# GpSimd takes over part of the weight conversion and of the float16 halves from ScalarE, and the first 680 pieces of the order are written anew

## The chip, the core and the metric

The kernel runs on one core of a Trainium2 chip. The metric is the device time in microseconds, the median of several runs. Five engines work side by side, each through a queue of its own that it empties in order: TensorE (PE, matmuls), VectorE (DVE), ScalarE (ACT), GpSimd (POOL) and SyncE (SP, which here only issues transfers). [...]

## The reference

Eight batches of an attention with 32 memory slots give x (4608 x 512, from q, k, v and phi), and two products with the gate h - tanh(h) between them follow:

```python
a = softmax(phi over the 576 positions)
k_m, v_m = a^T k, a^T v                     # 32 slots for each of 8 heads
x = softmax(q k_m^T / 8) v_m                # per head, then heads side by side
h = x @ w_in                                # 4608 x 512 @ 512 x 2048
out = (h - tanh(h)) @ w_out                 # @ 2048 x 512
```

w_in and w_out come as float64; all else is float32.

## The kernel before

The 4608 tokens are 18 units u of 256, and the 2048 hidden columns are 4 blocks fb of 512. For each batch b the product v_m w_in is formed first (steps `P`), so that one step `H u.fb` multiplies attention weights by it and gives h, and `M u.fb` adds one block of the second product. Every float32 operand of these products is split into two float16 halves, "high" and "low" (the rest), and three products of halves stand for one of floats. The halves of the weights are made once, at the start, from 32 raw blocks of 128 x 512 float64 values (i0 to i15 of w_in, o0 to o15 of w_out), taken in 16 pairs p.

All work stands in one order written out by hand as the string `ORDER`: about 1,700 pieces, read from left to right. A piece is a letter code with numbers, and a piece that is named several times goes on at each naming to its next part. The order of the pieces is the order of every engine's queue, and SP's too. The codes that matter here:

- `i3:pp5`, `o1:gg`: load a raw block, or a pair of blocks, into the buffer of that tag. `FX b` loads phi by rows (L151), `KA b` and `KB b` load k and v, `Q b.t` loads q. Blocks with the tag gg share a ring of three buffers.
- `T p`: converts a pair to float32. Its first part reads the top 16 bits of each value and writes them into the tile top (L453, ScalarE). Its second part joins them with shifted low words (L457, VectorE). Its third part writes the high half (L470, ScalarE).
- The low half of a pair: `Lv p` on VectorE (L481); `L p` scales on ScalarE (L493) and subtracts on GpSimd (L495); `Lp p` on TensorE (L487, L488) with a copy on ScalarE (L490).
- `X b`, `YX b`, `XT b`, `XU b`: maximum of phi (VectorE, L226), exponentials (ScalarE, L231), transposes on TensorE (L240, L251), each with a copy on ScalarE (L243, and L255 for the tail). `V b.r` pools k and v with them (TensorE, L267, L275). `N`, `U`, `S`, `AM`, `AE`, `AD`, `AT`, `AS` follow up to the halves of the attention weights. `AMv`, `ADv`, `ASv` are the same with VectorE in GpSimd's place.
- After `H`: the square (ScalarE, L633), `a` or `ap` (VectorE L646, ScalarE L648, VectorE L650), `g` the high half of the gate (ScalarE, L670), and `c` (GpSimd, L676) or `cv` (VectorE, L676) its low half.
- `Z0.0`: two matmuls whose result nobody reads (L862).

PSUM tiles of the steps rotate over two slots h0, h1 and a third tile pa; a piece that ends in x swaps the two kinds. The tile top has one buffer, under the tag us.

Of the kernel before, what the change touches and what calls it, by code (L numbers as in the profile page):

```python
# [81 lines left out]
H2.0x AT1.1 PL1.1 g0.1 FX2 Q2.1 OP1 ASv1.1 H2.0 T4 OP1 a2.0 X2 ASv1.1 c0.1 L5 FA2 i12:kv2 o11:gg i14:kv3 M0.1 H2.1 T12 OP0 H2.1 XP2 M0.1 a2.1 H3.0 H3.1x  # L82
Y2 CWv1 o14:kv3 o12:kv2 Q2.0 FA3 a2.0 a2.0 a2.1 OP0 T4 g2.0 c2.0 a2.1 YE2 T12 g2.1 W0 T12 M2.0 H3.0 c2.1 H3.1 T13 M2.0 M2.1 a3.0 a3.1 Lv12 Lv4
T13 V2.0 V2.1 P0.2x P1.2x a3.0 a3.1 OP2 T6 P0.2 a3.0 T6 N2 a3.1 PL0.2 g3.0 T13 W2 Lv13 M2.1 T7 H1.2x H0.2 g3.1 P1.2 T6 OP2 T7 c3.1 H1.2
H0.2 T7 c3.0 PL1.2 a1.2 a0.2 Lv7 Lv6 M3.0 U2x M3.0 M3.1 P0.3 T15 M3.1 a0.2 UV2 OP3 T15 BS0 a0.2 P0.3 g0.2 a1.2 PL0.3 a1.2 H1.3 H0.3x T14 g1.2
OP3 H1.3 U2 T15 M0.2 c0.2 M0.2 T14 ap1.3 cv1.2 ap1.3 H0.3 ap1.3 a0.3 UV2 S2.1x S2.0x P1.3 H2.2 S2.1 g1.3 T14 L14 P1.3 a0.3 L15 H2.2 S2.0 AM2.0 PL1.3
a0.3 M1.2 H2.3x H3.2 M1.2 c1.3 AM2.0 P2.0 L14 L15 M1.3 P2.1 M1.3 ap2.2 AE2.0 ap2.2 g0.3 H2.3 ap2.2 AMv2.1 AD2.0 a2.3 c0.3 AD2.0 BF0 H3.2 a2.3 P2.0 BH0 g2.2
BL0 a2.3 PL2.0 AMv2.1 AT2.0 ap3.2 cv2.2 R1 FQ3 P2.1 O1 O1 AE2.1 ap3.2 ap3.2 PL2.1 BS1 BF1 AS2.0 AS2.0 M0.3 M0.3 H4.0 H4.0 ap4.0 R0 P2.2 H3.3 g2.3 c2.3
O0 O0 BH1 BL1 AD2.1 AD2.1 ap4.0 ap4.0 M2.2 R2 X3 g3.2 c3.2 P2.2 PL2.2 H3.3 H4.1 H4.1 ap3.3 ap3.3 g4.0 ap4.1 ap4.1 KR3.0 XP3 Y3 f4.0 s4.0 M2.2 QT3.0
ap3.3 g3.3 s4.0 YE3 cv4.0 M2.3 M2.3 H4.2 O2 O2 c3.3 ap4.1 AT2.1 R3 H4.2 BS2 P2.3 AS2.1 P2.3 g4.1 AS2.1 V3.0x PL2.3 ap4.2 ap4.2 BF2 BH2 M3.2 f4.1 ap4.2  # L90
f4.2 M3.2 H4.3x s4.1 KR3.1 s4.1 BL2 V3.1 N3 k4:q XX M3.3 M3.3 H4.3 ap4.3 ap4.3 g4.2 U3x U3 UV3 M4.0 M4.0 cv4.1 UV3 S3.0x ap4.3 O3 O3 P3.0 M4.0
M4.0 S3.0 AMv3.0 P3.0 M4.1 H5.0 BS3 AMv3.0 AE3.0 f4.3 k0:e g4.3 cv4.3 M4.1 M4.1 M4.1 PL3.0 c4.2 s4.2 s4.2 P3.1 H5.0 a5.0 a5.0 M4.2 sv4.3 H5.1 CW4 BF3 a5.0
BH3 BL3 H5.1 g5.0 k2:q c5.0 M4.2 M4.2 f5.0 QT3.1 M4.2 H5.2 s5.0 sv4.3 M4.3 P3.1 a5.1 ADv3.0 a5.1 M4.3 M4.3 PL3.1 S3.1 ADv3.0 s5.0 a5.1 AT3.0 M4.3 H5.2 S3.1
E4 g5.1 a5.2 a5.2 E4 CW2 f5.1 E4 E4 sv5.1 P3.2 M4.3 H5.3 H5.3 FQ4 M5.0 FA4 M5.0 a5.2 cv5.1 E4 E4 AS3.0 a5.3 sv5.1 M5.0 M5.0 CW0 AS3.0 H6.0
M5.1 M5.1 M5.1 M5.1 f5.2 a5.3 g5.2 KR4.0 cv5.2 s5.2 s5.2 a5.3 H6.0 a6.0 f5.3 a6.0 a6.0 P3.2 H6.1 s5.3 H6.1 f6.0 M5.2 M5.2 M5.2 M5.2 P3.3 g5.3 c5.3 s5.3
M5.3 ap6.1 ap6.1 PL3.2 H6.2 ap6.1 g6.1 P3.3 AM3.1 AM3.1 c6.1 AE3.1 X4 XP4 g6.0 M5.3 c6.0 s6.0 PL3.3 f6.1 H6.2 a6.2 KR4.1 M5.3 Ev5 Ev5 M5.3 s6.0 Ev5 Ev5
Ev5 a6.2 ADv3.1 ADv3.1 YM4 M5.3 s6.1 Ev5 a6.2 YM4 YE4 H6.3 H6.3 s6.1 QT4.0 AT3.1 ap6.3 ap6.3 M6.0 M6.0 AS3.1 AS3.1 g6.2 k3:e f6.2 M6.0 sv6.2 V4.0 M6.1 M6.1
ap6.3 g6.3 f6.3 M6.0 M6.1 M6.1 sv6.3 sv6.2 H7.0 H7.0 a7.0 c6.2 V4.1 N4 W3 a7.0 sv6.3 M6.2 SI0 H7.1 a7.0 f7.0 H7.1 a7.1 U4 UV4 FQ5 UV4 M6.2 QT4.1
M6.2 a7.1 M6.2 U4 H7.2 H7.2 SSv0 NI0 a7.1 f7.1 a7.2 c6.3 M6.3 NI0 g7.0 a7.2 a7.2 s7.0 S4.0 c7.0 S4.0 AMv4.0 M6.3 M6.3 E6 s7.0 g7.2 c7.2 H7.3 H7.3
E6 a7.3 M6.3 E6 s7.1 E6 E6 W4 g7.1 M6.3 E6 s7.1 P4.0 P4.0 S4.1x S4.1 AMv4.1 a7.3 X5 CW3 AMv4.0 AE4.0 a7.3 g7.3 M7.0 M7.0 M7.0 M7.0 H8.0 H8.0  # L100
f7.2 c7.1 M7.1 M7.1 M7.1 M7.1 s7.2 f7.3 PL4.0 ap8.0 ap8.0 AMv4.1 AD4.0 ap8.0 XP5 s7.2 k5:e sv7.3 CW5 cv7.3 M7.2 KR5.0 AD4.0 f8.0 g8.0 M7.2 M7.2 M7.2 sv7.3 AE4.1
ADv4.1 s8.0 s8.0 c8.0 AT4.0 H8.1 YM5 ADv4.1 H8.1 P4.1 P4.1 M7.3 M7.3 a8.1 a8.1 a8.1 H8.2 AS4.0 PL4.1 M7.3 Ev7 H8.2 a8.2 FA5 QT5.0 YM5 a8.2 YE5 f8.1 M7.3
Ev7 P4.2 P4.2 g8.1 M7.3 AS4.0 c8.1 s8.1 s8.1 Ev7 Ev7 a8.2 g8.2 Ev7 H8.3 M8.0 Ev7 M8.0 c8.2 M8.0 V5.0 M8.1 AT4.1 AS4.1 KR5.1 PL4.2 H9.0 H8.3 a8.3 a8.3
a8.3 H9.0 f8.2 a9.0 a9.0 s8.2 s8.2 M8.1 M8.1 V5.1 f8.3 P4.3x P4.3 N5 s8.3 k6:e M8.0 M8.1 g8.3 H9.1x H9.1 a9.0 PL4.3 U5x s8.3 UV5 ap9.1 f9.0 M8.2 M8.2
UV5 ap9.1 ap9.1 c8.3 f9.1 M8.2 M8.2 M8.3 g9.0 c9.0 M8.3 SI1 k7:q SS1 U5 S5.0 g9.1 M8.3 sv9.0 k8:e E8 E8 H9.2 E8 E8 S5.0 M8.3 M8.3 AS4.1 H9.2
H9.3x sv9.0 CW6 ap9.2 ap9.2 ap9.2 QT5.1 c9.1 M9.0 M9.0 M9.0 E8 E8 s9.1 s9.1 AM5.0 H9.3 a9.3 AM5.0 f9.2 a9.3 FQ6 a9.3 NI1x NI1 AE5.0 AD5.0 AD5.0 H10.0x H10.0
M9.1 M9.1 a10.0 s9.2 P5.0 f9.3 S5.1x a10.0 g9.2 P5.0 c9.2 a10.0 M9.0 M9.1 H10.1 s9.2 CW8 M9.1 M9.2 g9.3 c9.3 S5.1 AMv5.1 AMv5.1 AE5.1 M9.2 M9.2 M9.2 AT5.0 AS5.0
X6 XP6 s9.3 H10.1 s9.3 M9.3 PL5.0 ap10.1 H10.2 AS5.0 ADv5.1 ap10.1 ap10.1 g10.1 f10.1 g10.0 YM6 f10.0 H10.2 a10.2 FA6 P5.1 P5.1 c10.0 CW7 YM6 PL5.1 M9.3 a10.2 a10.2
QT6.0 M9.3 M9.3 M9.3 s10.0 E9 E9 s10.1 H10.3x KR6.0 H10.3 H11.0 cv10.1 a10.3 E9 E9 E9 E9 a10.3 a10.3 YE6 P5.2 P5.2 s10.0 M10.0 M10.0 M10.0 KR6.1 V6.0 H11.0
# [1035 lines left out]
```

## Time and profile before

| | us |
|---|---|
| median of 3 runs | 633.12 |
| lowest and highest run | 632.84, 633.73 |
| the profiled execution, its own time | 633.45 |
| span in its profile, first to last instruction | 631.7 |

The span is 1.75 us shorter than the time of its own execution, and that execution is 0.33 us above the median. Every time of a row counts from the start of the span. In the notation `out<-in xcount` a number in square brackets is the time that the engine stood idle before the first instruction of the row, with what ended it.

### The profile page before, as it was taken

To read this page: it belongs to the slowest core of one execution; us is meant where nothing else is said; L and a number is where in the kernel's file an instruction comes from. 1 tells how busy PE (TensorE), PEld (TensorE's weight loads), DVE (VectorE), ACT (ScalarE), POOL (GpSimd) and SP (SyncE) were. 2 spreads that over 40 slices of the span, in tenths; PEclk is the share of its full clock that TensorE was granted. 3 is DMA by queue.
4 is the path that set the end of the run, shared out by engine and by line. 5 is a ranking of instruction groups with operands and counts; after the bars stand their busy time and mean duration, and the time that the engine had idled before them with its cause. 6 is when DMAs were issued, how large, how long until landed. Compare 5 with 4: busy or idle time off the path is not lost.

```text
span 631.7 us, 16308 instructions
## 1 busy us (share of the span) xinstructions
PE 618.8 (98%) x6924; PEld 487.2 (77%) x6924; DVE 546.1 (86%) x714; ACT 447.0 (71%) x623; POOL 344.1 (54%) x309
## 2 busy tenths in 40 slices
...
GB/s 341 400 371 357 152 204 146 164 40 68 189 141 166 39 95 60 67 147 128 100 117 91 140 41 156 102 90 173 38 46 168 123 102 79 56 147 34 167 101 39
DMA packets 25872, 85.02 MB, mean 135 GB/s; under 512 B 2752, under 2 KB 2752, under 8 KB 25024
## 3 DMA queue, kind: packets, MB, share of 16 engines
...
## 4 chain that ended last, share of the span: by engine, by line
PE 83%; DVE 9%; DMA 5%; ACT 1%; issue 1%; SPq 0%; POOL 0%; DVEq 0%; ACTq 0%; POOLq 0%
PE h L626 26%; PE x L773 22%; PE o L773 16%; PE o L754 7%; PE o1h L754 3%; PE pp L579 3%; DMA q<-in_qt_dram 2%; PE pkv L267 2%; DMA raw<-in_w_in_dram 1%; PE psc L319 1%; DMA raw<-in_w_out_dram 1%; DVE h L646 1%; DVE h L650 1%; DVE bw L713 1%; DVE bw L706 1%
## 5 line engine op out<-in xcount | busy, mean ns | idle before, releaser
L626 PEld LDWEIGHTS <-ph 128*128 128x128 f16 x2304 | 178.1, 98 | 20.2 <-issue 4.4
L676 POOL TENSOR_TENSOR g<-h,g 128x512 f16<-128x512 f32 x112 | 123.7, 1128 | 109.1 <-ACT g L670 109.1
L697 POOL TENSOR_TENSOR f<-s,f 128x512 f16<-128x512 f32 x86 | 107.9, 1276 | 84.5 <-ACT f L693 74.1
L773 PEld LDWEIGHTS <-f 128*128 128x128 f16 x1344 | 129.2, 98 | 20.2 <-issue 5.2
L626 PE MATMUL h<-ah,ph 128*128 128x256 f16 (+3 forms) x1536 | 138.7, 246 | 0.6 <-DVE h L646 0.6
L773 PE MATMUL x<-bt,f 128*128 128x256 f16 x1008 | 128.3, 273 | 0.0
L648 ACT ACTIVATE u<-u,beta 128x1024 f32<-128x1024 f32 x72 | 82.3, 1145 | 44.5 <-DVE h L646 44.3
L646 DVE SCALAR_TENSOR_TENSOR h<-h,u 128x1024 f32<-128x1024 f32 x72 | 87.8, 1222 | 26.6 <-ACT u L633 22.6
L633 ACT ACTIVATE u<-h 128x1024 f32<-128x1024 f32 x72 | 73.1, 1019 | 51.2 <-PE h L626 32.6
L773 PEld LDWEIGHTS <-g 128*128 128x128 f16 x1008 | 97.9, 98 | 14.7 <-issue 3.5
L650 DVE SCALAR_TENSOR_TENSOR h<-u,h 128x1024 f32<-128x1024 f32 x72 | 94.0, 1307 | 15.9 <-ACT u L648 15.7
L670 ACT ACTIVATE g<-h 128x512 f16<-128x512 f32 (+2 forms) x128 | 68.1, 579 | 14.7 <-DVE h L650 8.5
L626 PE MATMUL h<-al,ph 128*128 128x256 f16 (+3 forms) x768 | 75.1, 246 | 0.5 <-DVE al L570 0.5
L754 PEld LDWEIGHTS <-g 128*128 128x128 f16 x384 | 36.9, 98 | 43.7 <-issue 2.5
L693 ACT ACTIVATE f<-s 128x1024 f16<-128x1024 f32 x56 | 58.6, 1048 | 11.1 <-DVE s L686 7.0
L754 PE MATMUL o<-wout_hi,g 128*128 128x512 f16 x192 | 59.1, 379 | 0.0
L684 DVE TENSOR_TENSOR s<-h 128x512 f32<-128x512 f32 x56 | 45.7, 816 | 1.6
L773 PE MATMUL o<-wout_hi,f 128*128 128x256 f16 x224 | 45.9, 273 | 0.0
L773 PE MATMUL x<-wout_hi,g 128*128 128x256 f16 x224 | 45.8, 273 | 0.0
L773 PE MATMUL o<-wout_hi,g 128*128 128x256 f16 x224 | 45.8, 273 | 0.0
L773 PE MATMUL o<-bt,g 128*128 128x256 f16 x336 | 45.3, 273 | 0.0
L592 ACT ACTIVATE ph<-pp 128x1024 f16<-128x1024 f32 x32 | 32.5, 1015 | 12.8 <-PE pp L579 11.8
...
## 6 DMA issues: line engine op xcount, KB each, us to landing
...
raws<-in_w_in_dram SPq DMA_DIRECT2D x6, 1023.5 KB, 10.3
...
```

Of the source, the lines that this page charges most:

```text
L626: nc.tensor.matmul(hp[:, k, tu : tu + w], st[b]["p"][fb][i][:, g, cs], st[b][ax][:, g, ta : ta + w], start=(n == 0 and k % 2 == 0 and m == ...
L633: nc.scalar.activation(uu, hp, AF.Square, scale=1.0 / (S_A * S_P))
L646: nc.vector.scalar_tensor_tensor(t, hp, C2 * S_G / (S_A * S_P), uu, op0=ALU.mult, op1=ALU.mult)
L648: nc.scalar.activation(uu, uu, AF.Square, bias=c["beta"])
L650: nc.vector.scalar_tensor_tensor(h3, uu, CC, t, op0=ALU.add, op1=ALU.mult)
L670: nc.scalar.activation(hi, x, AF.Copy)
L676: eng.tensor_tensor(lo[:, ks], x[:, ks], hi[:, ks], op=ALU.subtract)
L684: nc.vector.tensor_tensor(s[:, 0:2], pair, a_block(h3, 0, 0).unsqueeze(1).to_broadcast((P, 2, 2, P)), op=ALU.add)
L693: nc.scalar.activation(f[:, 0], s, AF.Copy)
L697: eng.tensor_tensor(f[:, 1, ks], s[:, ks], f[:, 0, ks], op=ALU.subtract)
L754: nc.tensor.matmul(o, gx[:, k, P * tt : P * tt + P], wx[:, 4 * fb + k, :], start=(first and k == 0 and wx is wout_hi and gx is gh), stop=( ...
L773: nc.tensor.matmul(dst, a(na, kk), b(nb, kk), start=(new and kk == 0 and na == 0 and nb == 0), stop=(end and kk == 1 and na == 1))
```

## The change

Three things change.

- The first part of nine `T` (pairs 1, 2, 3, 7, 8, 9, 12, 14, 15) becomes a copy on GpSimd (`Tg`). The high half is cut off from `T` and becomes a piece of its own, `J` on ScalarE (12 pairs) or `Jg` on GpSimd (pairs 2, 6, 8, 13). Eight `g` (0.1, 0.3, 1.0, 1.3, 2.0, 2.1, 3.0, 3.1) become `gq`, copies on GpSimd. The tile top gets a second buffer under the tag bw, for pairs 2, 3, 8 and 10.
- The first 490 words of the order are replaced by 484 others; the 1,206 words from `N3 k4:q XX` on stay. Apart from the above, in the new words `L` remains for pairs 11 and 12 alone (before: 2, 5, 10, 11, 14, 15), `Lv` has eleven pairs (before seven), `cv` takes the place of `c` for 0.3, 3.0 and 3.1, some `AM`, `AD` and `AS` change between VectorE and GpSimd, four `a` become `ap` and two `ap` become `a`, and there are 15 `Z0.0` (before 28).
- The loads are issued in another order. Ahead of `Q0.0` stand the same loads as before.

```diff
-TOP = ("us",)
+TOP = ("us", "bw")
+TOP_B = (2, 3, 8, 10)
 
 ORDER = """
-i1:gg FX0 i0:gg Z0.0 T0 X0 i6:kv3 i2:gg i3:pp5 T0 i4:kv2 Z0.0 Z0.0 Z0.0 Z0.0 Z0.0 Z0.0 Z0.0 KA0 KB0 o2:gg Z0.0 YX0 T3 T0 o3:gg Z0.0 Z0.0 Z0.0 Z0.0 XT0 Z0.0
-Z0.0 T3 XU0 XT0 T1 T3 T1 Z0.0 Lp0 T2 XU0 T1 Lp3 Z0.0 Z0.0 Z0.0 V0.0 T2 Lv1 Z0.0 Z0.0 V0.1 Lp0 T2 L2 Lp3 T9 L2 N0 T9
-Q0.0 Q0.1 Z0.0 U0 Z0.0 UV0 U0 UV0 Z0.0 S0.0 T9 P0.0x S0.1 S0.0 AM0.0 AM0.0 P0.1 S0.1 AMv0.1 P0.0 P0.1 AE0.0 AMv0.1 AE0.1 AD0.0 AD0.0 AD0.1 AD0.1 AT0.0 PLp0.0
-PLp0.1 Z0.0 AT0.1 PLp0.1 Z0.0 Lp9x Z0.0 o6:gg o4:gg o5:pp2 i10:kv3 KB1 o7:gg PLp0.0 T10 ASv0.0 FX1 Lp9 ASv0.1 T10 ASv0.0 H0.0 ASv0.1 T10 T11 T11 H1.0x o10:pp5 o0:pp2 o1:gg
-L10 H0.0 KA1 i8:kv2 Q1.0 Q1.1 o8:gg KA2 o9:pp4 k1:q H1.0 KB2 H1.1 X1 YX1 L10 XT1 H0.1 T8 XU1 Z0.0 a0.0 a1.0 T8 a0.0 XT1 T8 XU1 V1.0 a0.0
-Lv8 V1.1 a1.0 g0.0 a1.0 M0.0 cv0.0 H1.1 ap1.1 N1 U1 M0.0 H0.1 g1.0 ap1.1 T11 UV1 U1 S1.0 ap1.1 UV1 a0.1 L11 S1.0 S1.1x T5 g1.1 a0.1 c1.0 L11
-S1.1 P1.1x P1.0 M1.0 AMv1.0 T5 T5 AM1.1 AMv1.0 P1.0 AE1.0 T4 L5 AM1.1 c1.1 PL1.0 AD1.0 AD1.0 AE1.1 AD1.1 AT1.0 W1 P1.1 ASv1.0 a0.1 ASv1.0 AD1.1 M1.0 M1.1 M1.1
...
+i1:gg i3:pp5 FX0 i0:gg i6:kv3 i4:kv2 i2:gg T0 KB0 KA0 o2:gg o3:gg Tg3 T0 X0 Tg3 Q0.0 J0 YX0 Tg2 J3 Tg1 Tg2 Q0.1 Lp0x Z0.0 Z0.0 Z0.0 Z0.0 XT0
+XU0x Z0.0 Z0.0 Lp3 Z0.0 Jg2 Tg1 Tg9 XT0 XU0 J1 Lp0 Lp3 Lv2 Lv2 Lv1 Lv1 Z0.0 Z0.0 V0.0 V0.1 N0 Z0.0 U0x Z0.0 UV0 U0 Z0.0 S0.0x Tg9
+UV0 S0.0 AM0.0 AM0.0 P0.0x S0.1x S0.1 AM0.1 P0.1x AM0.1 P0.0 J9 AE0.0 P0.1 AE0.1 AD0.0 AD0.0 AD0.1 AD0.1 AT0.0 AT0.1 o5:pp2 o4:gg o7:gg KA1 o6:gg Q1.1 Lp9x PLp0.1 PLp0.0
+Z0.0 Z0.0 T10 Lp9 ASv0.0 T10 ASv0.0 PLp0.0 H0.0x FX1 PLp0.1 ASv0.1 ASv0.1 J10 o1:gg T11 o0:pp2 Tg8 H0.0 H1.0 H1.1 Lv10 Lv10 T11 H1.0 o9:pp4 Q1.0 KB1 X1 a0.0
+a1.0 YX1 Tg8 i8:kv2 o10:pp5 i10:kv3 KB2 o11:gg FQ3 XT1 Jg8 H0.1 XU1 a0.0 XT1 a0.0 a1.0 XU1 Z0.0 V1.0 g0.0 H1.1 J11 V1.1 Lv8 Lv8 a1.0 M0.0 cv0.0 ap1.1
...
-    def to_f32(p, ts):
+    def to_f32(p, ts, pool):
 
         r = [raws.pop(2 * p + i) for i in range(2)]
         if "top" not in c:
             c["top"] = [big.tile([P, 2, 512], U32, tag=TOP[i], name=f"top{i}", bufs=1) for i in range(len(TOP))]
             for x in c["top"]:
                 nc.gpsimd.memset(x, 0)
-        top = c["top"][0]
-        c["top"].append(c["top"].pop(0))
+        top = c["top"][p in TOP_B]
         if len(r[0].shape) == 3:
             parts = [(r[0], top, ts)]
         else:
...
         dims = {2: ("p (f w) -> p f w",), 3: ("p i (f w) -> p i f w",)}
         for x, g, t in parts:
             e = dims[len(x.shape)][0]
-            nc.scalar.activation(g.bitcast(F16).rearrange(e, w=2)[..., 1], x.bitcast(BF16).rearrange(e, w=4)[..., 2], AF.Copy)
+            half, bits = g.bitcast(F16).rearrange(e, w=2)[..., 1], x.bitcast(BF16).rearrange(e, w=4)[..., 2]
+            if pool:
+                nc.gpsimd.tensor_copy(half, bits)
+            else:
+                nc.scalar.activation(half, bits, AF.Copy)
         yield
         for x, g, t in parts:
             e = dims[len(x.shape)][0]
...
 
     tfs, his = {}, {}
 
-    def conv(p):
+    def conv(p, pool=False):
 
         ts = big.tile([P, 2, 512], U32, tag="ss", name=f"wt{p}")
-        yield from to_f32(p, ts)
-        yield
+        yield from to_f32(p, ts, pool)
         tfs[p] = ts.bitcast(F32)
+
+    def high(p, pool=False):
         his[p] = half_of(p, win_hi, wout_hi)
-        nc.scalar.activation(his[p], tfs[p], AF.Copy, scale=S_W)
+        if pool:
+            nc.gpsimd.tensor_scalar(his[p], tfs[p], S_W, None, op0=ALU.mult)
+        else:
+            nc.scalar.activation(his[p], tfs[p], AF.Copy, scale=S_W)
 
     def half_of(p, win, wout):
         f, o = 2 * p % 4, 2 * p - 16
...
         return half_of(p, win_lo, wout_lo)
 
     def low(p):
+        yield
         nc.vector.scalar_tensor_tensor(low_of(p), tfs[p], S_W, his[p], op0=ALU.mult, op1=ALU.subtract)
 
     def low_pe(p):
...
             (a_block(h3, 1, 0), [a_block(gg[:, n], 1, 0) for n in range(2)]),
         )
 
-    def a_high(u, fb):
+    def a_high(u, fb, pool=False):
         gs[u, fb] = big.tile([P, 2, 4, UT], F16, tag="gg", name=f"g{u}{fb}", bufs=3)
         for x, (hi, _) in a_parts(u, fb):
-            nc.scalar.activation(hi, x, AF.Copy)
+            if pool:
+                nc.gpsimd.tensor_copy(hi, x)
+            else:
+                nc.scalar.activation(hi, x, AF.Copy)
 
     def a_low(u, fb, eng):
         for x, (hi, lo) in a_parts(u, fb):
...
         "AD": lambda b, t: att.soft_div(b, st[b], t), "ADv": lambda b, t: att.soft_div(b, st[b], t, nc.vector),
         "AT": lambda b, t: att.soft_turn(b, st[b], t), "AS": lambda b, t: att_split(b, t, nc.gpsimd), "ASv": lambda b, t: att_split(b, t, nc.vector),
         "Z": warm, "P": att_p, "PL": att_pl, "PLp": att_pl_pe, "H": mm1, "a": lambda u, fb: cubic(u, fb, False), "ap": lambda u, fb: cubic(u, fb, True),
-        "g": a_high, "c": lambda u, fb: a_low(u, fb, nc.gpsimd), "cv": lambda u, fb: a_low(u, fb, nc.vector), "f": s_forms, "s": s_high, "sv": lambda u, fb: s_high(u, fb, nc.vector),
-        "T": conv, "L": low_pool, "Lv": low, "Lp": low_pe,
+        "g": a_high, "gq": lambda u, fb: a_high(u, fb, True), "c": lambda u, fb: a_low(u, fb, nc.gpsimd), "cv": lambda u, fb: a_low(u, fb, nc.vector), "f": s_forms, "s": s_high, "sv": lambda u, fb: s_high(u, fb, nc.vector),
+        "T": conv, "Tg": lambda p: conv(p, True), "J": high, "Jg": lambda p: high(p, True), "L": low_pool, "Lv": low, "Lp": low_pe,
         "BS": b_sum, "BF": b_form, "BH": b_high, "BL": b_low,
         "SI": squares_in, "NI": norms_in, "SO": squares_out, "NO": norms_out, "SS": squares_sum, "SSv": lambda i: squares_sum(i, nc.vector), "CW": window, "CWv": lambda k: window(k, nc.vector),
         "GG": lambda: check(tc, c, big), "GX": lambda: check_all(tc, c, place), "XX": steady, "WD": flag,
```

## Rows read from the trace of the kernel before

**Rows 1.** The page's first lines: span, and busy time of an engine with its share.

```profile
span 631.7 us, 16308 instructions
...
PE 618.8 (98%) x6924; PEld 487.2 (77%) x6924; DVE 546.1 (86%) x714; ACT 447.0 (71%) x623; POOL 344.1 (54%) x309
```

**Rows 2.** All waits of TensorE from 52 us on: total us, times, longest.

```profile
PE h L626 <- DVE h L646: 0.6, 1, 0.6
```

**Rows 3.** Chain that ended last, 20 to 52 us: start, length, what.

```profile
11.66 14.49 DMA q<-in_qt_dram
...
26.29 0.79 PE psc L319 x16
```

**Rows 4.** Busy time by stretch: PE, PEld, DVE, ACT, POOL, granted clock, DMA.

```profile
26.00:52.00 26.00, 23.96 (x334) 16.37 (x335) 21.07 (x30) 23.42 (x30) 5.61 (x4) 1.00 0.98 381
52.00:191.00 139.00, 138.91 (x1424) 85.41 (x1422) 123.46 (x142) 105.06 (x126) 67.88 (x50) 1.00 0.44 155
191.00:216.00 25.00, 24.38 (x254) 19.16 (x253) 24.23 (x34) 15.57 (x22) 13.68 (x12) 1.00 0.34 114
```

**Rows 5.** TensorE in order of time, 31 to 52 us: start, length, [idle before <-releaser].

```profile
31.30 1.03 PE L862 MATMUL warm<-nid 128*128 128x512 f16 x4
...
34.88 0.59 PE L862 MATMUL warm<-nid 128*128 128x512 f16 x2
...
47.98 0.44 PE L251 MATMUL pkv<-ident,pt 128*128 128x128 f32 x2 [0.44 <-ACT e L243]
48.25 0.59 PE L862 MATMUL warm<-nid 128*128 128x512 f16 x2
49.36 1.98 PE L267 MATMUL pkv<-kv,e 128*32 128x129 f32 x64 [0.52 <-ACT e L255]
...
51.66 0.39 PE L754 MATMUL o<-wout_hi,g 128*128 128x512 f16 x1
```

**Rows 6.** ScalarE in order of time, 42 to 50 us.

```profile
42.38 1.43 ACT L231 ACTIVATE pt<-pt,mx 128x576 f32<-128x576 f32 x2
43.72 0.78 ACT L453 ACTIVATE top<-raw 128x512 f16<-128x512 bf16 x1
45.24 0.78 ACT L453 ACTIVATE top<-raw 128x512 f16<-128x512 bf16 x1 [0.75 <-DMA raw<-in_w_out_dram]
45.89 1.12 ACT L648 ACTIVATE u<-u,beta 128x1024 f32<-128x1024 f32 x1
46.92 1.00 ACT L243 ACTIVATE e<-pet 128x1024 f32<-128x1024 f32 x1
47.82 1.05 ACT L470 ACTIVATE wout_hi<-wt 128x1024 f16<-128x1024 f32 x1
48.77 0.54 ACT L255 ACTIVATE e<-pkv 64x128 f32<-64x128 f32 x2
```

**Rows 7.** Issue of the second phi tile on SP's queue, in order of time.

```profile
35.90 0.33 SPq L151 DMA_DIRECT2D pt<-in_phx_dram  x1
```

**Rows 8.** Groups by form: count | busy us, mean ns | idle before.

```profile
L453 ACT ACTIVATE top<-raws 128x1024 f16<-128x1024 bf16 x8 | 11.0, 1370 | 1.6 <-DVE wt L457 1.4 <-DMA raws<-in_w_out_dram 0.2
L481 DVE SCALAR_TENSOR_TENSOR win_lo<-wt,win_hi 128x1024 f16<-128x1024 f32 x4 | 4.8, 1219 | 0.2 <-ACT win_hi L470 0.2
```

**Rows 9.** Groups of GpSimd by form, same columns.

```profile
L495 POOL TENSOR_TENSOR wout_lo<-wt,wout_hi 128x1024 f16<-128x1024 f32 x4 | 9.5, 2384 | 6.3 <-ACT wt L493 6.3
...
L443 POOL MEMSET top<- 128x1024 uint32 x1 | 1.0, 952 | 0.0
masks.py:199 POOL TENSOR_SCALAR_AFFINE_SELECT ident<-ident 128x128 f32<-128x128 f32 x1 | 0.3, 293 | 0.1
```

**Rows 10.** VectorE in order of time, 24 to 41 us.

```profile
24.03 1.14 DVE L457 SCALAR_TENSOR_TENSOR wt<-raw,top 128x512 uint32<-128x512 uint32 x1 [0.38 <-ACT top L453]
25.61 0.69 DVE L457 SCALAR_TENSOR_TENSOR wt<-raw,top 128x512 uint32<-128x512 uint32 x1 [0.45 <-ACT top L453]
...
40.09 1.34 DVE L226 TENSOR_REDUCE mx<-pt 128x2 f32<-128x1152 f32 x1
```

**Rows 11.** GpSimd in order of time, 20 to 30 us.

```profile
22.48 2.13 POOL L495 TENSOR_TENSOR win_lo<-wt,win_hi 128x1024 f16<-128x1024 f32 x1 [19.80 <-ACT wt L493]
```

More of the change, by code (lines that the diff above doesn't have):

```diff
@@ L82 @@
[L82 to L109, printed above, removed]
@@ new lines @@
+J4 OP1 QT3.0 i12:kv2 KA2 i14:kv3 J5 k1:q H2.0 ASv1.1 OP0 Tg12 Q2.1 o12:kv2 o14:kv3 a2.0 Lv4 Lv4 ASv1.1 OP1 a2.0 H2.1 Tg12 a2.0 Lv5 Lv5 ap2.1 W0 J12 M0.1
+H3.0x H3.1 gq2.0 ap2.1 H3.0 OP0 H3.1 T13 X2 ap2.1 c2.0 gq2.1 ap3.1 c2.1 ap3.0 T13 XP2x M2.0 M2.0 M2.1 Y2 ap3.1 ap3.0 L12 YE2 V2.0x V2.1 ap3.1 ap3.0 T6
+T6 P0.2 P1.2x L12 Jg13 P0.2 gq3.1 Jg6 OP2 P1.2 Tg7 gq3.0 CWv1 N2 PL0.2 Lv6 Lv6 Tg7 PL1.2 Tg15 cv3.0 M2.1 H1.2x H0.2 U2x M3.0 M3.0 OP2 W1 J7
+U2 S2.0x H0.2 UV2 H1.2 cv3.1 Lv13 Lv13 UV2 a1.2 a0.2 Lv7 Lv7 P0.3x S2.1 P1.3x S2.0 a1.2 P0.3 a0.2 P1.3 Tg15 M3.1 PL0.3 AM2.0 a1.2 H1.3 M3.1 PL1.3 S2.1
```

70 lines of the change are left out of this document (48 added, 22 removed).

## The prediction

> **What bounds the kernel now.** I read the page first, then TensorE's waits, then the chain, then stretches of time. TensorE is busy for 618.8 of the span of 631.7 us [rows 1]. A busy TensorE is not yet a full one, so the waits decide: from 52 us to the end it waits for another engine once, for 0.6 us [rows 2]. So nothing that only relieves another engine after 52 us can gain more than that 0.6; any new wait of TensorE there is a loss, since there is no slack to take it up. The first matmul of the second product, M0.0, starts at 51.66 us [rows 5]. The question is whether the new order brings it forward, and whether TensorE stays fed behind it.
>
> The chain splits the time before 51.66. The tile of q lands at 26.16 (issued at 11.66, under way for 14.49 us), and the scores S0.0 start at 26.29 [rows 3]. The same loads stand ahead of Q0.0 in both orders, so I let S0.0 start where it does now. It may come up to 0.5 us later, since the idle matmuls at the very start are gone and Lp0 is now TensorE's first work; H0.0 then still has to wait for the softmax and the halves of it, and the same chain sets it.
>
> Between S0.0 and M0.0 lie 25.4 us. TensorE is idle for 2.04 of the 26 us from 26 to 52, some 0.3 of that before S0.0 [rows 4]. Eight matmuls of that stretch do nothing (four at 31.30, two at 34.88, two at 48.25); two more of them lengthen a row from 0.59 to 1.03, so one is 0.22 and eight are 1.8 [rows 5]. The front can therefore give at most 1.75 + 1.8 = 3.5 us.
>
> **The change part by part.** *ScalarE before M0.0.* TensorE's pieces from H1.1 to V1.0 keep their order: H1.1, XT1, H0.1, XU1, Z, V1.0. The old order has two waits there. XU1 waits 0.44 us for the copy of XT1, and V1.0 waits 0.52 for the tail copy of XU1 [rows 5]. Both copies are late because ScalarE's queue holds other work before them. YX1 ends at 42.38 + 1.43 = 43.81; then come the first top of pair 8, 0.75 us of waiting for its second block, the second top (to 46.02), the square of a0.0, and only at 46.92 the copy. Behind that the high half of pair 8 (47.82, 1.05 us) holds up the tail copy until 48.77 [rows 6]. In the new order pair 8 is on GpSimd in both its parts. Between YX1 and the copy stands one square: 43.8 + 1.1 + 1.0 gives 45.9, before TensorE needs it. TensorE was ready for XU1 at 47.98 - 0.44 = 47.54; its two transposes take to 47.8, the tail copy 0.54 more, and V1.0 starts near 48.45 in place of 49.36. That is 0.9 us.
>
> *Against it in the same place.* FX1 still cannot be issued before AT0.1 has freed its buffer (issue at 35.90 now [rows 7]). X1 starts at 40.09 and ends at 41.43 [rows 10], and ScalarE takes it up at 42.38 [rows 6], so X1 may be 0.95 us later for nothing. The new order puts Lv10 before it, 1.22 us [rows 8], and thereby J10 on ScalarE. That is 0.3 too long; I count 0.1 of it as lost, the rest behind H1.1. The front gives 0.9 - 0.1 = 0.8 us. Bounds: 0, if X1 comes a whole microsecond later than that, and 3.5, if every idle moment above were filled. I stay near the row that I can follow.
>
> *The softmax of batch 0.* AM0.1 moves to GpSimd behind AM0.0, T9's and T10's work on ScalarE changes place, and two Z stand before H0.0 where three stood after P0.1. I find no piece that brings H0.0 forward and none that holds it back by more than some tenths: 0, bounds -0.5 and +0.5.
>
> *ScalarE later.* Nine tops at 1.37 us [rows 8] leave it, and four high halves, eight g and four scalings of about 1.05 each (as the high half [rows 6]): 9 x 1.37 + 16 x 1.05 = 29 us. After 52 us TensorE does not wait for ScalarE [rows 2], so this is worth 0 by itself.
>
> *GpSimd.* It gets 21 passes over 1024 columns: nine tops, four high halves, eight g. No such copy is in the trace. Below, a fill of 1024 columns takes 0.95 us and reads nothing; above, the subtraction of low halves takes 2.38 and reads two tiles; a one-input pass over 128 columns takes 0.29, whose eightfold is 2.3, start included [rows 9]. I take 1.65 for 1024, the middle of the ends. Seven passes fall before 52 us, where GpSimd is busy 5.6 of 26 us. Fourteen fall behind it: 14 x 1.65 = 23 us, less two L and three c of about 2.4 each, so +11 us on 67.9 of 139 [rows 4]. It has the room at 2.38 too. Of its new work gq stands closest to TensorE; M2.0 and M3.0 follow their gq by several pieces. 0, at either end.
>
> *VectorE.* Four low halves come from GpSimd (1.22 each [rows 8]) and three low halves of g, which I price like them: 7 x 1.22 = 8.5 us. The moves of softmax passes cancel to less than one pass: 0. The seven spread over 52 to 191 us, where VectorE has 139 - 123.5 = 15.5 us free [rows 4]. From 191 to 216 only 0.8 are free, but there the order is the old one.
>
> *Collisions.* A join of 512 columns takes 0.69 us, and 1.14 when it starts at 24.03 inside GpSimd's pass of 22.48 to 24.61 [rows 10, 11]: +0.45. If half of the fourteen passes meet one such instruction it is 3.2 us. So VectorE gets 8.5 + 3.2 = 11.7 us, and 15.5 are free. I take 0 for TensorE; the ends are 0 and what the second rival says.
>
> The Trainium skill (SBUF — State Buffer, section Who interferes with whom) states that a VectorE instruction with two SBUF inputs and a GpSimd instruction that reads SBUF shut each other out, and the second waits for the whole of the first. The longer join agrees with it. By that rule, with every one of the fourteen passes blocking for 1.65 us, an estimate of 23 us would stand where I count 3.2, and VectorE would no longer fit.
>
> *The second top.* It costs one more fill, 0.95 us at the start of GpSimd [rows 9], while nothing has landed that it could use. 0.
>
> **The sum.** In the profiled execution M0.0 moves from 51.66 to 50.9 and the rest follows unbroken: span 631.7 - 0.8 = 630.9, its time 633.45 - 0.8 = 632.65. That execution is 0.33 above the median of the three runs, so the median should be 633.12 - 0.8 = 632.3 us.
>
> **The rivals.** *The front is filled better than I can follow.* For: ScalarE is busy for 23.4 of the 26 us from 26 to 52 [rows 4], and five pairs of tops and two high halves leave it in the first 52 us; the eight idle matmuls need not be waited for either. Against: the chain from 26.16 runs over q, the softmax and its halves, which the change does not shorten. If two thirds of the 3.5 us are saved, the time is 633.1 - 2.4 = 630.7.
>
> *VectorE no longer keeps up (slower).* Place: 100 to 190 us, where it gets the low halves of pairs 6, 13, 14, 15 and of g3.0 and g3.1. For: in the stretch before 216 it is busy for 24.2 of 25 us [rows 4], and the one wait of TensorE is for it [rows 2]. Part of its free time is waiting for ScalarE and TensorE, which no order removes; say two thirds of 15.5 are usable, 10.4. The point from which it decides is when the additions pass that. At 11.7 TensorE is late by 1.3 us; with all fourteen passes colliding at 0.45 the additions are 14.8 and it is late by 4.4. In the middle, 2.9: 632.3 + 2.9 = 635.2. Against: ahead of 160 us the new order has several microseconds between such a piece and TensorE's need of it.
>
> *The front gains nothing.* X1 stands behind Lv10 and T11, as above; with a further 0.7 us there, YX1, XT1 and V1.0 are as late as now, and the rest is unchanged: 633.1. The same holds if S0.0 comes later by a microsecond, for instance because o2 and o3, and with them Q0.0, are issued later.
>
> **How the numbers follow.** A measurement of this kernel tells about 0.2% from no change, 1.3 us. My forecast (632.3, its own range 631.4 to 633.0) gets 0.42, the better filled front 0.24, VectorE late 0.21, no gain 0.13. Faster by over 0.2% (below 631.85) are the second case and three tenths of the first: 0.24 + 0.13 = 0.37. Slower (above 634.4) is the third: 0.21. Within are the rest: 0.42. The range goes from 630.3 (leaving out some 0.07 of the filled front) to 635.2 (half of the third case, 0.1).
>
> **What the profile would show.** Right: S0.0 within 0.5 us of 26.3; the copy of XT1 on ScalarE right after one square; V1.0 near 48.5 and M0.0 near 50.9; TensorE's waits after that still under 1 us; GpSimd's copies between 0.95 and 2.4 us. Wrong: waits of TensorE for VectorE's L646, L650 or low halves between 90 and 190 us; joins of over 2 us beside GpSimd's copies; or M0.0 at 49.5 or earlier.

## The result: the new order and engines cost 4.5 us, most of it before 62 us

The changed kernel takes 637.7 us (median of four runs, 637.04 to 637.88) against 632.98 for the kernel before beside it: ratio 1.0071, 95% interval 1.0054 to 1.0088, which is 4.5 us. The forecast was 632.3 with a range up to 635.2. The profiled execution has 637.04 us and a span of 635.2. A profile shows one execution: this one lies 0.7 us below the median of its kernel, and those of r5, r7, r8 and r11 below lie 0.9 to 1.2 above theirs. The part of the order that was written anew is 490 words, 484 in the new kernel, and not the 680 of the title.

The page's line of busy times of the changed kernel, which answers to [rows 1]:

```profile
PE 613.4 (97%) x6898; PEld 484.9 (76%) x6898; DVE 553.2 (87%) x720; ACT 422.1 (66%) x594; POOL 366.9 (58%) x326
```

ScalarE lost 24.9 us and GpSimd gained 22.8, as the change intends. TensorE is 5.4 us less busy in a longer span. The second stretch of [rows 4] in the changed kernel (columns as there):

```profile
52.00:191.00 139.00, 136.67 (x1437) 84.08 (x1426) 127.04 (x143) 86.97 (x107) 76.14 (x56) 1.00 0.47 164
```

From 52 to 191 us TensorE is idle for 2.3 us where it was idle for 0.1. All its waits from 52 us on, which answer to [rows 2]:

```profile
PE ptr L308 <- DVE kvn L285: 0.9, 1, 0.9
PE h L635 <- DVE h L655: 0.6, 1, 0.6
PE h L635 <- DVE pr L861: 0.4, 1, 0.4
PE psc L320 <- issue: 0.4, 1, 0.4
PE psc L320 <- DVE h L655: 0.4, 1, 0.4
PE psc L320 <- ACT u L657: 0.3, 1, 0.3
PE pp L588 <- DVE h L655: 0.2, 1, 0.2
```

The 0.9 and the first two of psc (0.4 each) stand between 57 and 62 us: U1 and the first pieces of S1. That is one loss, 1.7 us. The other is the start. The chain that ended last in the changed kernel, 2 to 29 us (start, length, what), which answers to [rows 3]:

```profile
2.10 7.40 DMA raw<-in_w_in_dram
...
11.14 2.08 PE pw L496 x2
...
15.78 2.17 PE warm L874 x8
...
23.63 3.31 DVE win_lo L490 x2
```

The chain no longer runs over q. Pair 0's second block lands at 9.50 us, its join on VectorE ends at 11.10, and TensorE has no work before 11.14. Lp0, its first, then takes until 15.57, 4.4 us; in the trace of before such a piece takes 2.15 us (from 12.97). The granted clock of that stretch nevertheless reads 1.00 (columns as [rows 4]):

```profile
11.10:13.20 2.10, 2.06 (x3) 0.84 (x4) 1.88 (x2) 1.24 (x2) 0.99 (x1) 1.00 1.02 415
```

Behind Lp0 come the idle matmuls that the new order has there, Lp3, and two low halves on VectorE (pairs 2 and 1). These hold up N0, which stands behind them. Alone two would take 2.44 us [rows 8]; here they start just after GpSimd's tops of pair 9 and take 3.39, of which the chain shows 3.31:

```profile
23.09 2.82 POOL L455 CAST top<-raw 128x512 f16<-128x512 bf16 x2 [1.84 <-DVE wt L461]
```

```profile
23.55 3.39 DVE L490 SCALAR_TENSOR_TENSOR win_lo<-wt,win_hi 128x1024 f16<-128x1024 f32 x2
```

TensorE in order of time, as [rows 5], here of the changed kernel:

```profile
23.57 1.98 PE L268 MATMUL pkv<-kv,e 128*32 128x129 f32 x64
...
27.68 0.43 PE L308 MATMUL ptr<-ident,kvn 128*128 128x128 f32 x2 [1.21 <-DVE kvn L285]
...
28.91 0.72 PE L320 MATMUL psc<-q,kT 64*32 64x288 f32 x16
...
37.78 1.91 PE L635 MATMUL h<-ah,ph 128*128 128x256 f16 x16
...
50.84 1.98 PE L268 MATMUL pkv<-kv,e 128*32 128x129 f32 x64 [0.21 <-ACT e L256]
...
53.13 0.39 PE L766 MATMUL o<-wout_hi,g 128*128 128x512 f16 x1
```

S0.0 starts at 28.91 against 26.29, 2.6 us late, and V1.0 at 50.84 against 49.36, 1.5 late. So between them 1.1 us were gained, and two losses stand around that gain. M0.0 starts at 53.13, 1.5 us late; the other 2.0 us of the 3.5 between the two spans arise behind it. The medians are a microsecond further apart than the two profiled executions, and no trace of the changed kernel shows where.

The second loss, on GpSimd and on VectorE in order of time in the changed kernel (pair 8, ahead of and behind M0.0):

```profile
48.34 3.67 POOL L476 TENSOR_SCALAR wout_hi<-wt 128x1024 f16<-128x1024 f32 x1 [1.18 <-DVE wt L461]
```

```profile
52.05 1.23 DVE L490 SCALAR_TENSOR_TENSOR wout_lo<-wt,wout_hi 128x1024 f16<-128x1024 f32 x1 [2.66 <-POOL wout_hi L476]
...
56.98 0.49 DVE L285 TENSOR_TENSOR kvn<-pkv,kr 128x128 f32<-128x128 f32 x2
```

VectorE stands still for 2.66 us until GpSimd has made pair 8's high half. The products of the gate's polynomial and the normalized sums N1 (L281 to L285) queue behind it, and U1 and S1 wait for these. The new operations of GpSimd, 0 to 216 us, by form (columns as [rows 9]):

```profile
L680 POOL CAST g<-h 128x1024 f16<-128x1024 f32 x8 | 11.0, 1371 | 16.7 <-PE o1h L766 9.3 <-DVE h L659 7.4
...
L455 POOL CAST top<-raws 128x1024 f16<-128x1024 bf16 x5 | 6.7, 1344 | 19.7 <-DMA raws<-in_w_in_dram 8.7 <-DMA raws<-in_w_out_dram 6.0 <-DVE wt L461 5.0
L476 POOL TENSOR_SCALAR wout_hi<-wt 128x1024 f16<-128x1024 f32 x2 | 6.4, 3222 | 1.2 <-DVE wt L461 1.2
...
L476 POOL TENSOR_SCALAR win_hi<-wt 128x1024 f16<-128x1024 f32 x2 | 5.5, 2768 | 0.0
...
L504 POOL TENSOR_TENSOR wout_lo<-wt,wout_hi 128x1024 f16<-128x1024 f32 x2 | 4.3, 2143 | 4.0 <-ACT wt L502 4.0
```

### The profile page after: what moved, and what is told of

It reads as the page before. It is cut to its first block, busy times and chain, and to the rows that moved or that the text cites. A ratio compares the mean times of both kernels' runs of the same rounds, so it can differ in the third digit from the quotient of the medians.

```text
span 635.2 us, 16247 instructions
## 1 busy us (share of the span) xinstructions
PE 613.4 (97%) x6898; PEld 484.9 (76%) x6898; DVE 553.2 (87%) x720; ACT 422.1 (66%) x594; POOL 366.9 (58%) x326
## 4 chain that ended last, share of the span: by engine, by line
PE 75%; DVE 13%; POOL 4%; issue 3%; ACT 3%; DMA 1%; SPq 0%; ACTq 0%; DVEq 0%; POOLq 0%
PE h L635 23%; PE x L785 22%; PE o L785 16%; PE o L766 5%; PE pp L588 3%; DVE h L655 2%; PE o1h L766 2%; PE pkv L268 2%; DVE h L659 2%; DVE wt L461 1%; DVE win_lo L490 1%; DMA raw<-in_w_in_dram 1%; POOL g L688 1%; PE psc L320 1%; POOL wout_hi L476 1%
## 5 line engine op out<-in xcount | busy, mean ns | idle before, releaser
L688 POOL TENSOR_TENSOR g<-h,g 128x512 f16<-128x512 f32 x106 | 114.9, 1105 | 71.2 <-ACT g L682 70.9
L709 POOL TENSOR_TENSOR f<-s,f 128x512 f16<-128x512 f32 x86 | 109.4, 1293 | 79.2 <-ACT f L705 74.3
L682 ACT ACTIVATE g<-h 128x512 f16<-128x512 f32 (+1 forms) x120 | 59.6, 548 | 12.1 <-DVE h L659 6.9
L601 ACT ACTIVATE ph<-pp 128x1024 f16<-128x1024 f32 x32 | 32.5, 1016 | 23.5 <-PE pp L588 18.0
```

What stands on the lines that cost most here:

```text
L682: nc.scalar.activation(hi, x, AF.Copy)
L688: eng.tensor_tensor(lo[:, ks], x[:, ks], hi[:, ks], op=ALU.subtract)
L709: eng.tensor_tensor(f[:, 1, ks], s[:, ks], f[:, 0, ks], op=ALU.subtract)
```

## The experiments

Changes of time below are a kernel's ratio to the kernel before beside it, times 633 us; the intervals are some 0.5 to 1.1 us to either side. Names with a number (r4) are those of the expectations. Of the order only words that change are shown, with cuts marked by dots.

**The two halves of the change apart.** r2 keeps the old order and gives it the new engines for tops, high halves and activations, with the low halves where the old order has them; r3 keeps the new order and returns most work to ScalarE. (The new order with every engine as before was not tried.) Of r2 two pairs and two of the eight `g` are shown.

```diff
 r2 (old order)
-T3 ... T3 ... T3     T2 ... T2 ... T2      g1.0 ... g0.1
+Tg3 ... Tg3 ... J3   Tg2 ... Tg2 ... Jg2   gq1.0 ... gq0.1
 r3 (new order)
-Tg7 Tg8 Tg12 Tg14 Tg15  Jg2 Jg6 Jg8 Jg13  gq0.1 ... gq3.1
+T7 T8 T12 T14 T15       J2 J6 J8 J13      g0.1 ... g3.1
```

> The old order word for word, with the same engine for each piece as in the change: nine tops, four weight halves and eight g on GpSimd, two buffers of top; the low halves, softmax passes, loads and idle matmuls stay as in the old order. First theory (the order of the front is the main loss, the engines cost only where a scaled copy stands on a chain): S0.0 within 0.5 us of 26.3, time 633 to 635. Rival (GpSimd's passes slow VectorE by themselves): S0.0 near 26.3 as well, but TensorE waits for VectorE by 2 to 5 us after 52 us and the time is 635 to 638.

> The new order, with the tops of pairs 7, 8, 12, 14, 15, the four weight halves and the eight g back on ScalarE; GpSimd keeps the tops of pairs 1, 2, 3 and 9. First theory: S0.0 is still 2.4 us or more late (28.5 to 29), so the time stays above 634.5, best guess 635.5; what is gained against the changed kernel is the loss after 52 us. Rival (the engines cause the whole loss): 633 or less, as the front's order costs nothing.

r2: 645.9 us, ratio 1.0193 (1.0180 to 1.0206). S0.0 starts at 26.50, on time, but TensorE then waits again and again; the largest sum is for low halves of activations:

```profile
PE o L766 <- POOL g L688: 2.2, 3, 1.6
```

r3: 659.2 us, ratio 1.0411 (1.0396 to 1.0426); S0.0 at 29.13, and ScalarE is late throughout, as in this row of its waits:

```profile
PE o L766 <- ACT ot L849: 3.4, 1, 3.4
```

So the late start comes with the new order, and neither half is good without the other: r2 loses 12 us, r3 (with four of the nine tops still on GpSimd) 26. The places of S0.0 were near those expected, the times were not: r2 lies 8 us beyond both of its theories, and r3 24 above its best guess.

**Pair 8's high half, and the others, back to ScalarE.**

```diff
-Jg2 ... Jg8 ... Jg13 ... Jg6
+J2 ... J8 ... J13 ... J6
```

> The new kernel with the four weight halves Jg 2, 6, 8, 13 made on ScalarE again (J); all else as changed. First theory (two separate losses: TensorE's first pieces make S0.0 2.6 us late, and the 2.8 to 3.7 us of a scaled copy on GpSimd hold Lv8, and with it N1 and S1, on VectorE): TensorE's waits of 0.85 before U1 and 0.77 before S1.0 and S1.1 vanish, S0.0 stays near 28.9, and the time falls from 637.7 by 1.0 to 1.8 to about 636.2. Rival (VectorE is simply overloaded by low halves and collisions between 52 and 191 us): the waits move elsewhere, 637.3 or more.

637.7 us, ratio 1.0076 (1.0061 to 1.0091): nothing gained. The waits for N1 and in S1 are gone, but ScalarE now makes XU1 wait 1.22 us and V1.0 0.61, and V1.0 starts at 52.99. The two microseconds moved ahead of V1.0. The time is the rival's, its cause (an overloaded VectorE) is not: my expectation had taken ScalarE's free time for room.

**Idle matmuls first.** Thirteen words Z0.0 behind the first load, ahead of Lp0.

```diff
-i1:gg i3:pp5 FX0 i0:gg ...
+i1:gg Z0.0 (13 times) i3:pp5 FX0 i0:gg ...
```

> The new kernel with 13 idle pieces Z0.0 put ahead of Lp0, as the old order has them. First theory (the slow start of TensorE and what stands behind it make S0.0 late): Lp0 takes 2.2 in place of 4.6 us, V0 ends 2 us or more earlier, S0.0 at 26.3 to 27.2, time 635.4 to 636.2. Rival (VectorE's two low halves ahead of N0, held up by GpSimd's tops of pair 9, set U0 and S0.0): S0.0 still 28.5 or later, time 637.3 or more.

635.7 us, ratio 1.0032 (1.0019 to 1.0044): +2.0 in place of +4.5. TensorE in order of time in this run:

```profile
3.69 8.48 PE L874 MATMUL warm<-nid 128*128 128x512 f16 x26 [3.69 <-DVE nid L1102]
12.01 1.02 PE L496 MATMUL pw<-wt,idw 128*128 128x512 f32 x2
...
21.85 1.98 PE L268 MATMUL pkv<-kv,e 128*32 128x129 f32 x64
...
25.15 0.44 PE L308 MATMUL ptr<-ident,kvn 128*128 128x128 f32 x2 [0.40 <-DVE kvn L285]
...
26.39 0.72 PE L320 MATMUL psc<-q,kT 64*32 64x288 f32 x16
28.62 0.72 PE L320 MATMUL psc<-q,kT 64*32 64x288 f32 x16 [0.87 <-DMA q<-in_qt_dram]
...
48.91 1.98 PE L268 MATMUL pkv<-kv,e 128*32 128x129 f32 x64 [0.21 <-ACT e L256]
```

Lp0's matmuls of 512 columns take 1.02 us for two where they took 2.08, though the piece starts 0.9 us later than in the changed kernel. S0.0 is back at 26.39 and V1.0 0.45 us ahead of the kernel before. That the idle matmuls bring this is shown. They bring it in two ways. V0.0 starts 1.7 us earlier (21.85 against 23.57): that is TensorE's own work. The other 0.8 us of S0.0's 2.5 come from VectorE, as TensorE waits 0.40 us for N0 in place of 1.21. On VectorE and GpSimd in this run:

```profile
21.83 2.44 DVE L490 SCALAR_TENSOR_TENSOR win_lo<-wt,win_hi 128x1024 f16<-128x1024 f32 x2
```

```profile
23.22 2.34 POOL L455 CAST top<-raw 128x512 f16<-128x512 bf16 x2 [1.77 <-DMA raw<-in_w_out_dram]
```

The two low halves still overlap GpSimd's tops of pair 9, but now the second of them starts first, at 23.05, and the first top is the longer one (1.66 us, the second 0.76). So this part hangs on a small shift between two engines, which nobody planned.

**Pair 8 in four forms, with the idle matmuls first.** r5 has pair 8's high half on ScalarE, r6 all four, r8 pair 8's tops too. r7 leaves the scale out of GpSimd's high halves.

```diff
 r5
-Jg8
+J8
 r6
-Jg2 Jg8 Jg13 Jg6
+J2 J8 J13 J6
 r8
-Tg8 Tg8 Jg8
+T8 T8 J8
 r7
-nc.gpsimd.tensor_scalar(his[p], tfs[p], S_W, None, op0=ALU.mult)
+nc.gpsimd.tensor_copy(his[p], tfs[p])
```

> The changed kernel with thirteen idle matmuls ahead of TensorE's first work, and in addition the high half of pair 8 alone made by ScalarE (about 1.05 us) in place of GpSimd (3.7 us). Theory (the scaled copy of pair 8 on GpSimd holds the low half on VectorE, and that holds N1, U1 and the first pieces of S1): VectorE takes up the low half of pair 8 with no wait for GpSimd, TensorE's waits between 52 and 62 us (about 1.9 us in the kernel with the idle matmuls alone) go, V1.0 comes at most 0.4 us later (near 49.2), and the time is 633.6 to 634.2 us, 1.5 to 2 below that kernel's 635.7. Rival (ScalarE has no room for it before 52 us, as when all four went back without the idle matmuls): V1.0 comes 1 us or more later and the time stays at 635.2 to 636.

> The same idle matmuls, and all four high halves on ScalarE. Theory (only pair 8's stands close enough to TensorE; the other three scaled copies of GpSimd, near 2.8 us each, are covered): within 0.4 us of the kernel with pair 8's alone on ScalarE, 633.4 to 634.3. Rival (the others cost too): a further 0.5 to 1.5 us down, 632 to 633.

> The same idle matmuls, and GpSimd makes the four high halves with its plain copy instead of the multiplication by the scale; the scale of those halves is left out, so their products have other values, and the instruction and its place are all that the time tells. Theory (the multiplication by a constant is what makes GpSimd's pass 2.8 to 3.7 us): the four passes take 1.0 to 1.5 us like its copies of h, VectorE's low half of pair 8 waits at most 0.4 us, and the time is 633.5 to 634.3. Rival (collisions with VectorE make it, whatever the operation): the passes stay above 2.5 us and the time at 635.4 to 636.

> The same idle matmuls, and pair 8 wholly on ScalarE, tops and high half, in the new order. Theory (taking pair 8 off ScalarE is what brings V1.0 forward, step b of the prediction): V1.0 is 0.8 to 1.6 us later than the 48.91 of the kernel with the idle matmuls alone, and the time is 0.5 to 1.5 above that of the kernel with the high half alone on ScalarE: 634.3 to 635.5. Rival (ScalarE has room for both): V1.0 within 0.5 us of that and the times equal within 0.3 us.

r7: 633.5 us, ratio 0.9993 (0.9985 to 1.0002), 2.5 us below r4. The pass of pair 8 on GpSimd, and those of pairs 2 and 6, in r7:

```profile
47.35 1.97 POOL L476 CAST wout_hi<-wt 128x1024 f16<-128x1024 f32 x1 [1.16 <-DVE wt L461]
```

```profile
L476 POOL CAST win_hi<-wt 128x1024 f16<-128x1024 f32 x2 | 2.1, 1036 | 1.2 <-DVE wt L461 1.2
```

Same tiles, same place: 3.67 became 1.97, and where nothing collides 2.77 became 1.04. So the multiplication costs GpSimd 1.7 us a pass, and pair 8's takes 0.9 more in either form; VectorE's low half then still waits 0.94 us, more than the 0.4 expected. In both kernels a product of VectorE of 1.2 us starts 0.1 to 0.2 us before pair 8's pass. That the 0.9 are a collision with it is argued, not shown.

The other three missed. r5 fell on the side of its rival; r6 lies 5 us above its theory and 6 above its rival, r8 4 above the upper end of its theory. r5: 636.1, ratio 1.0037 (1.0024 to 1.0050), no gain on r4; TensorE waits 1.8 us for ScalarE's copy of XT1. Three of its stretches, columns as [rows 4]:

```profile
48.00:50.00 2.00, 0.23 (x2) 0.23 (x3) 1.16 (x2) 2.00 (x3) 0.00 (x0) 1.00 0.97 397
50.00:52.00 2.00, 1.39 (x20) 0.83 (x22) 2.00 (x3) 1.97 (x4) 0.00 (x0) 0.72 1.02 401
52.00:54.00 2.00, 2.00 (x44) 1.83 (x40) 2.00 (x3) 1.98 (x3) 1.53 (x1) 0.50 1.01 405
```

After the stretch in which TensorE was nearly idle, the granted clock is 0.50 for 52 to 54 us, its lower level of 1.2 GHz, and V1.0's 64 matmuls take 3.42 us instead of 1.98. In this execution one wait on ScalarE is paid for twice; whether the others of r5 paid the second time is open. r6: 639.3, ratio 1.0094 (1.0078 to 1.0109); Lp3 waits a further 2.0 us for the copy of XT0, which stands behind pair 2's high half on ScalarE, the low halves on VectorE take 3.39 us again, S0.0 is at 29.21, so that what the idle matmuls gave is lost, and V1.0 is slow too (3.28 us). r8: 639.3, ratio 1.0086 (1.0073 to 1.0099). ScalarE in r8:

```profile
44.24 1.39 ACT L457 ACTIVATE top<-raw 128x512 f16<-128x512 bf16 x2 [3.79 <-DMA raw<-in_w_out_dram]
```

In the new order pair 8's block lands so late that its top holds ScalarE's queue for 3.79 us, with two squares and YX1 behind it; XT1 then waits 3.5 us, V1.0 starts at 55.55, and the granted clock is 0.50 from 48 to 52 us. So in this order pair 8's tops do not belong on ScalarE: r8 stands 3.2 us above r5, more than the 0.75 us of waiting that [rows 6] showed.

**Pair 8's high half on VectorE**, with the idle matmuls (r9) and without (r12); the other three stay on GpSimd.

```diff
-Jg8
+Jv8
 def high(p, pool=False):
...
+    if pool is nc.vector:
+        nc.vector.tensor_scalar(his[p], tfs[p], S_W, None, op0=ALU.mult)
```

> The changed kernel with the thirteen idle matmuls first, and pair 8's high half made by VectorE, with the scale, in place of GpSimd; the other three stay on GpSimd. Theory (what costs is the wait of VectorE for GpSimd's scaled copy, 2.67 us, and ScalarE has no room for it either): the pass takes VectorE 0.6 to 1.3 us, its low half of pair 8 follows with no wait, the waits of TensorE for the normalized sums (0.9) and for the low half (0.4) go, V1.0 stays near 48.9 us, and the time is 633.2 to 634.0 us, as with the plain copy on GpSimd (633.5). Rival (VectorE has no room before 52 us either): 634.8 to 635.8.

> The changed kernel as it is, without the idle matmuls at the start, and pair 8's high half on VectorE alone. Theory (two separate losses, the start of TensorE and the scaled copy of pair 8): S0.0 stays at 28.9 and V1.0 near 50.8, the waits after 52 us go, and the time is 635.3 to 636.1, about 2 below 637.7. Rival (the two share one cause, the late start): 637.0 to 638.

r9: 633.9 us, ratio 1.0005 (0.9995 to 1.0016). r12: 636.1, ratio 1.0042 (1.0030 to 1.0054), S0.0 at 29.23. VectorE in r9:

```profile
46.68 0.69 DVE L476 TENSOR_SCALAR wout_hi<-wt 128x1024 f16<-128x1024 f32 x1
...
48.42 1.22 DVE L492 SCALAR_TENSOR_TENSOR wout_lo<-wt,wout_hi 128x1024 f16<-128x1024 f32 x1
```

The pass takes VectorE 0.69 us, and the 2.66 us of waiting are gone; both times lie where the theories had them. The two causes add up. Against the kernel before, the changed kernel stands at +4.5, with the idle matmuls at +2.0, with this pass at +2.7, and with both at +0.3: 2.5 or 2.4 for the one, 1.8 or 1.7 for the other.

**Looking for a faster version.** r10 issues q ahead of pair 9's blocks and drops the idle matmuls around U0. r11 loads pair 0's blocks in the old sequence and drops the idle matmuls ahead of H0.0. Both start from r9.

```diff
 r10
-o2:gg o3:gg ... Q0.0 ... Q0.1       U0x Z0.0 UV0 U0 Z0.0 S0.0x
+Q0.0 Q0.1 o2:gg o3:gg               U0x UV0 U0 S0.0x
 r11
-i1:gg Z0.0 (13) i3:pp5 FX0 i0:gg    PLp0.0 Z0.0 Z0.0 T10
+i1:gg FX0 i0:gg Z0.0 (13) i3:pp5    PLp0.0 T10
```

> The same, with both transfers of q of batch 0 issued ahead of the two of pair 9's blocks, which wait for a buffer, and without the four idle matmuls on either side of U0. Theory (the scores start when q has landed and U0 is there, and what then follows from S0.0 to V1.0 moves with them): q lands 1 to 2.5 us earlier, S0.0 starts at 25.5 to 25.9 in place of 26.4, S0.1 no longer waits 0.9 for q, V1.0 comes 0.4 to 1 us earlier, and the time is 632.2 to 633.3. Rival (pair 9 comes later and takes the gain back, or the first rows of batch 1 set V1.0 by their own load): no more than 0.2 us down, 633.2 to 634.2.

> The kernel with the idle matmuls first and pair 8's high half on VectorE, and in addition the first blocks of pair 0 and the first rows loaded ahead of pair 3's block, as in the kernel before, and no idle matmuls ahead of H0.0 (0.9 us). Theory (the late first join of pair 0 delays the buffers that the transfers of pair 9 wait for, and with them q; S0.1 then sets the softmax): o2 is issued 1 us earlier or more, the 0.83 us of S0.1's wait for q shrink below 0.3, H0.0 starts at 34.8 to 35.5 in place of 36.03, V1.0 at 48.0 to 48.6 in place of 48.92, and the time is 632.6 to 633.5. Rival (the transfers land by their bytes, whatever the issue, or batch 1's first rows set V1.0): S0.1 and V1.0 within 0.3 us of where they are, 633.4 to 634.3.

r10: 637.2 us, ratio 1.0060 (1.0048 to 1.0073), worse than either theory. S0.0 comes only 0.3 us earlier, now waiting for ScalarE's kT. Pair 9's blocks land later, VectorE's joins of them stand ahead of batch 0's vl in its queue, and TensorE waits for vl:

```profile
30.37 0.63 PE L590 MATMUL pp<-win_hi,vl 64*32 64x512 f16 x8 [3.33 <-DVE vl L564]
```

r11: 632.9 us, ratio 0.9986 (0.9977 to 0.9994), inside the range of its theory. The blocks of pair 9 are issued at 9.43 in place of 11.3, and S0.1 at 27.87 no longer waits; V1.0 starts at 48.64 and M0.0 at 51.42. S0.0 is 0.3 later than in r9. It is the one version whose whole interval lies below the kernel before, by 0.9 us: less than the 0.2% that the forecast had called a change. The two edits in it were not told apart, and where its 0.9 us against r9's +0.3 come from is open: V1.0 is 0.28 earlier than in r9, but M0.0 is 0.2 later (51.21 in r9), since V1.1 waits 0.28 for its rows; and that execution is 1.1 us above r11's median.

## Why the prediction was wrong, point by point

**The start of S0.0: wrong, and the larger loss.** The step that failed is "The same loads stand ahead of Q0.0 in both orders, so I let S0.0 start where it does now", with up to 0.5 us for the missing idle matmuls. It followed only the link of the chain that ended last, the landing of q. In the trace of before TensorE stood idle ahead of S0.0, for q:

```profile
26.29 0.72 PE L319 MATMUL psc<-q,kT 64*32 64x288 f32 x16 [1.40 <-DMA q<-in_qt_dram]
```

Those 1.40 us were all the room of TensorE's own chain over Lp0, Lp3, N0 and U0. That chain came some 4.0 us later (28.91 against 26.29 - 1.40) and became the longer one: 1.4 were hidden, 2.6 were measured at S0.0. The idle matmuls give 2.4 to 2.5 us of time back; at S0.0 in r4 that is 1.7 through TensorE's slow first work and 0.8 through the low halves behind GpSimd's tops, a collision that the prediction had looked for only behind 52 us. In the sum I had idle matmuls only as time that could be saved.

**ScalarE before M0.0: right.** H0.0 of the kernel before:

```profile
35.37 1.91 PE L626 MATMUL h<-ah,ph 128*128 128x256 f16 x16
```

From there to V1.0 it takes 13.99 us and the changed kernel 13.06: 0.93 gained where 0.9 were worked out. The 0.1 set against it for X1 did not show: YX1 starts 7.04 us behind H0.0, in the kernel before 7.01. The copy of XT1 stands behind one square, as predicted. ScalarE in the changed kernel, against [rows 6]:

```profile
44.82 1.43 ACT L232 ACTIVATE pt<-pt,mx 128x576 f32<-128x576 f32 x2
46.16 1.15 ACT L657 ACTIVATE u<-u,beta 128x1024 f32<-128x1024 f32 x1
47.40 1.02 ACT L244 ACTIVATE e<-pet 128x1024 f32<-128x1024 f32 x1
...
50.23 0.55 ACT L256 ACTIVATE e<-pkv 64x128 f32<-64x128 f32 x2 [0.78 <-PE pkv L252]
```

**The softmax of batch 0: right.** S0.0 to H0.0 is 8.87 us against 9.08, inside the bound of half a microsecond. With the 0.93 that is the 1.1 us gained.

**GpSimd's passes: wrong for one kind, and in what depends on it.** The means of tops (1.34) and activations (1.37) lie inside 0.95 to 2.38 us; the scaled high half does not, with 2.77 at the least and 3.67 for pair 8. I had capped a one-input pass by a two-input subtraction, and the subtraction is the cheaper (2.14 in this kernel). The second failure is "0, at either end": I looked for TensorE behind gq, and the pass that stood closest was Jg8, with Lv8 behind it on VectorE and N1 behind that. It is worth 1.7 to 1.8 us, as r9 and r12 show.

**VectorE: the sum was too large, and the rival was not what happened.** VectorE is busy for 127.0 us from 52 to 191, 3.6 more, and over the whole span for 7.1 more, not 11.7. The seven low halves cost what was priced, collisions included (11.5 us): eleven of weights take 16.7 us where seven took 8.5, and six of g 7.2 where three took 3.9. But two of them (pairs 2 and 10) fall ahead of 52 us, and the joins, which I had let grow, take 21.4 us in the whole span where they took 23.5. From 100 to 191 us TensorE waits twice, 0.3 us for ScalarE and 0.4, ahead of 150.15, for VectorE's L861. Those 0.4 are what there is of the rival; the time passed its 635.2 by another way. Where a collision costs time, it is on the path by position: 3.31 us for two low halves beside GpSimd's tops. The first of them started when 0.72 us of a top were left and took 0.51 longer than alone. The Trainium skill (SBUF — State Buffer, Who interferes with whom) states that of a VectorE instruction with two SBUF inputs and a GpSimd instruction that reads SBUF the first shuts the other out; that row agrees in kind. The sum of 23 us that the prediction worked out by it did not occur.

**The rival that came nearest in kind** was "the front gains nothing", which named S0.0 a microsecond late and gave 633.1 (the late VectorE, at 635.2, was nearer in time). It named the symptom. The cause that it gave, a later issue of q (12.12 us against 11.66), was not what held S0.0, which does not wait for q in the changed kernel.
